# A tensor kept in DRAM between two passes: rows by feature, or blocks by tokens

## The chip, the core and the metric

The kernel runs on one core of one Trainium2 chip. The metric is the device time of one launch in microseconds (us), as the median of the runs shown. The engines are named as the profile names them: PE (TensorE, matmuls) with PEld (its weight loads), DVE (VectorE), ACT (ScalarE), POOL (GpSimd), SP (SyncE, which here only issues DMAs).

## What is computed

The kernel computes a block's output and all of its gradients in one launch: a layer norm of x (2048 tokens, 512 features), a long convolution over the tokens whose kernel comes from a state-space model (128 states per feature), a feed-forward network, and a gate.

```
xn = layernorm(A_u)
s  = causal_conv(xn, K) + xn * Dskip        # K from A, B, C, dt; by FFT in the reference
h  = xn @ w1                                # 2048 x 1792
o  = silu(h) @ w2                           # 2048 x 512
y  = A_u + s * silu(o)
outputs: y, and the gradients of A_u, A, B, C, log_dt, Dskip, w1, w2 for a given grad_out
```

What matters here is h, the inner tensor of the feed-forward network. It is made in the forward pass and needed twice more in the backward pass: its silu' for dh, and silu(h) for the gradient of w2. All inputs and outputs are bf16.

## The kernel before

h is 2048 x 1792 in bf16, 7.3 MB. It is too much to keep beside the rest, so it goes to DRAM, in the tensor `Hd`. With features on the partitions, h consists of FT = 14 row blocks of 128 features (`ft`), and its 2048 tokens are taken in eight chunks (`c`) of 256. `Hd` has the shape [14, 128, 2048]: for one row block and one partition, all 2048 tokens lie in one run of 4096 bytes. Four places touch it:

- **The store** (`gen_ffn_fwd`, line 1403). The forward network goes over the eight chunks. In each, 14 row blocks of `ps_h` are computed by matmuls and copied into `hT`, first eight blocks, then six. After each part ACT makes `aT` = silu(`hT`) for the second matmul (`ps_o`), and POOL issues the store of `hT` (`k.st` is `nc.gpsimd.dma_start`). A store writes, for every partition, 8 or 6 runs of 256 tokens, which is 512 bytes each. `hT` is single-buffered for each of the two parts.
- **The loads for da** (`gen_ffn_da`, line 1708). They read the same parts back into `dhT`, again in 512-byte runs; ACT replaces them by silu'(h), DVE multiplies by `ps_da`, and the product goes to DRAM as `DHd` and, as weights, into the matmuls `ps_dx`. Three buffers of eight row blocks and two of six allow loading ahead.
- **The plain loads for the gradient of w2** (`gen_dw2`, line 1764), eleven of the 14 row blocks. One load brings a row block with all its 2048 tokens into `h_in`, one run of 4096 bytes per partition. PE transposes it in 16 pieces of 128 x 128 (`pt_t`), ACT applies silu into `a_tok`, and 16 matmuls (`ps_w2`, shown as `ps_w<-YD,a_tok`) sum over the tokens.
- **The transposing loads** of the same stage (line 1762), for ft = 9, 11, 13. The DMA transposes [128, 2048] into `h_in`, and PE has no part in it.

`h_in` has two buffers; `load(ft + 2)` is recorded while ft is worked on. Its pool `fw` takes memory that the da stage (pools `wt` and `da`) uses before.

`DHd`, the stored dh, already has the shape [8, 128, 14, 256], with each partition's rows of a chunk contiguous, and `dh_tok<-DHd` reads it back with a transposing DMA whose source is [1024, 256].

All loads and the transposes go through SP's queue, in order; the stores of h, `Od` and most outputs go through POOL's.

The order of the work on each engine is not the order of the code. The functions only record operations; the class `Plan` then lays out a schedule from costs of its own. `backward` gives every operation a latest start; `forward` lets each engine take, among what is ready, the operation with the earliest one; the resulting list per engine is fixed by `tie`. `FIRST` and `LAST` hold its five settings: how long before its latest start a DMA may be issued (`hold`, ns), how far ACT may reach past an operation that needs another table (`table`) and PE past one of another tile shape (`turn`), the reluctance to use the slower of two possible engines (`shy`), and the time from a DMA's last byte to its landing (`land`). `ROUNDS` passes of the two refine it, `FROM` seeds the first, and `NUDGES` shifts the latest starts of chosen operations by pseudo-random amounts: 630 entries of seed, kind and size, found by a search that was done before the kernel was written down.

```
if "DMA" in kind or "Dma" in kind:
    ...
    run = min(self.run(a) for a in (aps[0], aps[1])) * 2
    packets = total / run
    each = 7.6 + run / 24.4 if run > 1024 else 25 if run <= 256 else 30.8 if run <= 512 else 48
    issue = (540.0 if packets <= 512 else 900.0) if eng == "Pool" else 600.0 if total < 200000 and run == 512 else 330.0 if packets <= 256 else 400.0
    return issue, packets * each / 16
...
self.lead = [400.0 + (c[0] if e == "Pool" else min(c[0], 330.0)) for c, e in zip(self.cost, self.eng)]
...
line = max(line, t + self.lead[n]) + l      # in forward, for a DMA
done[n] = line + land
```

Of the kernel before, what the change touches and what calls it, by code (L numbers as in the profile page):

```python
# [20 lines left out]
P = 128  # L21
# [159 lines left out]
class Plan:  # L181
# [5 lines left out]
    FROM, ROUNDS = (649172052, 1, 0), 5  # L187
    FIRST, LAST = (30000.0, 1500.0, 1500.0, 120.0, 3500.0), (30000.0, 1500.0, 1500.0, 120.0, 3500.0)
    NUDGES = [(2732807006, 5, 2000), (3483623756, 4, 500), (36678232, 7, 1000), (3625006935, 3, 100), (1835227684, 0, 100),
# [1190 lines left out]
def gen_ffn_fwd(k):  # L1380
    nc, fp = k.nc, k.fp
    D, FT, DK, T = k.D, k.FT, k.DK, k.T
    for c in range(T // 2):
# [3 lines left out]
        for f in range(FT // 2):  # L1387
# [12 lines left out]
            if f in (3, 6):  # L1400
                f0, n = (0, 8) if f == 3 else (8, 6)
                nc.scalar.activation(out=aT[:, f0:f0 + n], in_=hT[:, 0:n], func=ACT.Silu)
                k.st(k.Hd[f0:f0 + n, :, cs].rearrange("f p n -> p f n"), hT[:, 0:n])
# [668 lines left out]
```

## Time and profile before

| | |
|---|---|
| time of the runs, median of 3 | 562.91 us (562.78 to 563.13) |
| profiled execution, its time | 562.31 us |
| its span, first to last instruction | 560.6 us |
| mean granted TensorE clock | 0.991 |
| busy: PE, DVE, ACT, POOL | 515.5, 508.1, 432.0, 69.4 us |
| DMA packets | 178,882, 137.77 MB |

The profile is of one execution. Its stages, by what PE does: to about 42 us the layer norm, the tables and the constants; to 200 us the forward network together with the convolution forward; to 250 us the end of the convolution, the gates and the start of the backward pass; to 380 us the convolution backward together with da and dx; to about 450 us the state-space gradients; from 412 us on the weight gradients, first of w2 and then of w1, with the layer norm's backward pass. All operations are recorded by one helper, so every row carries the same line number, 171, and the tile's name tells what it is. "busy" of PE is taken from pipelined matmuls with modelled ends. A wait is put down to what came last. The chain of waits is followed back from the last instruction; a stage in which two engines are equally full can appear in it under either.

### The profile page before, as it was taken

Reading aid. Unit: us, or ns where it says so; the run is one execution under the profiler, and the core shown is the slowest. Engines: PE = TensorE matmul, PEld = TensorE weight load, DVE = VectorE, ACT = ScalarE, POOL = GpSimd, SP = SyncE. Lnnn points to the kernel's source line nnn. Section 1 sums busy time; section 2 is a strip of 40 time slices with the busy share of each in tenths; the row PEclk is TensorE's granted clock in tenths of the full one; section 3 lists DMA queues with packets and bytes.
Section 4 is the critical chain, followed back from the end, with each engine's and each line's share of the span. In section 5 each row is a group of like instructions: output and inputs, shape, how many; then the busy total and the mean of one; then the engine's idle time right before and its main releaser. Section 6 shows DMA issues by size and latency. Waiting matters only on the chain.

```text
span 560.6 us, 14249 instructions
## 1 busy us (share of the span) xinstructions
PE 515.5 (92%) x5820; PEld 380.5 (68%) x5820; DVE 508.1 (91%) x866; ACT 432.0 (77%) x726; POOL 69.4 (12%) x138
## 2 busy tenths in 40 slices
PE   1698999999989997889999999999969999999997
PEld 1465677868657666565877667778657687778775
DVE  9989999999999799999999999649999999999932
ACT  8989899999989889989878878247367665785621
POOL 5131111100100100000000100000000303301142
PEclk9999999999999998999999999999989999999999
DMA  8996959997999999985498997997999999998893
GB/s 236 270 354 179 291 191 337 246 335 155 237 350 280 359 337 218 236 208 169 156 236 295 252 329 234 188 264 180 229 254 241 227 237 277 256 229 217 200 233 109
DMA packets 178882, 137.77 MB, mean 246 GB/s; under 512 B 125121, under 2 KB 158657, under 8 KB 176257
## 3 DMA queue, kind: packets, MB, share of 16 engines
q1 hardware_dynamic: 172384, 118.77, 82.5%
q0 software_dynamic: 6144, 17.83, 9.6%
q8 instruction: 45, 0.74, 0.5%
q10 hardware_dynamic: 288, 0.26, 0.2%
q14 instruction: 21, 0.16, 0.1%
HBM read 50.07 MB, written 56.63 MB: 190 GB/s over the span
## 4 chain that ended last, share of the span: by engine, by line
PE 58%; DVE 16%; ACT 13%; DMA 8%; issue 3%; SPq 2%; POOL 0%; DVEq 0%; ACTq 0%; POOLq 0%
PE ps_w L171 18%; PE ps_da L171 8%; PE ps_i L171 7%; PE ps_dx L171 6%; DMA dB<-dA 4%; PE ps_s L171 4%; PE ps_o L171 3%; ACT mag_all L171 3%; PE ps_h L171 3%; PE pt_t L171 3%; PE psS L171 3%; PE ps_v L171 2%; ACT dA L171 2%; DVE AR L171 2%; DVE dA L171 2%
## 5 line engine op out<-in xcount | busy, mean ns | idle before, releaser
L171 PEld LDWEIGHTS <-W 128*128 128x128 bf16 x952 | 88.1, 99 | 22.9 <-issue 7.4
L171 ACT CAST dA<-ps_s 128x512 bf16<-128x512 f32 x160 | 86.2, 641 | 9.2 <-PE ps_s L171 6.3
L171 PE MATMUL ps_o<-W,aT 128*128 128x512 bf16 x224 | 59.0, 379 | 2.9 <-ACT aT L171 2.9
L171 PEld LDWEIGHTS <-xn 128*128 128x128 bf16 x512 | 47.3, 99 | 20.1 <-DVE xn L171 13.0
L171 PE MATMUL ps_da<-doT,W 128*128 128x256 bf16 x448 | 59.7, 273 | 0.8 <-DVE doT L171 0.8
L171 PE MATMUL ps_h<-XT,W 128*128 128x256 bf16 x448 | 58.9, 277 | 1.3 <-DVE dA L171 0.8
L171 PE MATMUL ps_w<-YD,a_tok 128*128 128x512 bf16 x224 | 57.5, 382 | 0.0
L171 PE MATMUL ps_w<-dh_tok,xn 128*128 128x256 bf16 x448 | 57.1, 273 | 0.0
L171 ACT CAST Vb<-ps_v 128x336 bf16<-128x336 f32 x109 | 40.6, 459 | 21.2 <-PE ps_v L171 15.5
L171 PE MATMUL ps_dx<-W,dhT 128*128 128x512 bf16 x224 | 55.2, 379 | 0.0
L171 ACT CAST dB<-ps_i 128x512 bf16<-128x512 f32 x82 | 45.3, 647 | 4.5 <-PE ps_i L171 4.3
L171 DVE TENSOR_TENSOR dhT<-ps_da,dhT 128x512 bf16<-128x512 f32 x56 | 37.8, 685 | 6.1 <-PE ps_da L171 5.9
L171 PEld LDWEIGHTS <-TF 128*128 128x128 bf16 x416 | 28.5, 100 | 12.5 <-ACT TF L171 5.3
L171 PEld LDWEIGHTS <-YD 128*128 128x128 bf16 x576 | 28.4, 98 | 9.0 <-DVE YD L171 1.7
L171 PEld LDWEIGHTS <-dhT 128*128 128x128 bf16 x224 | 20.7, 98 | 20.1 <-issue 1.2
L171 PEld LDWEIGHTS <-a_tok 128*128 128x128 bf16 x224 | 21.3, 99 | 16.9 <-issue 0.5
L171 PEld LDWEIGHTS <-aT 128*128 128x128 bf16 x224 | 19.4, 98 | 19.5 <-ACT aT L171 3.4
L171 PE MATMUL ps_v<-Gb,YT 128*128 128x168 bf16 x256 | 31.1, 242 | 1.3 <-DVE Gb L171 0.7
L171 ACT CAST o<-ps_w 128x512 bf16<-128x512 f32 (+1 forms) x27 | 15.1, 559 | 20.9 <-PE ps_w L171 20.4
L171 PE MATMUL ps_s<-dB,F 128*64 128x512 bf16 x192 | 28.6, 400 | 2.8 <-DMA dB<-dA 1.7
L171 POOL DMA_DIRECT2D out_dram<-o x20 | 12.3, 616 | 142.8 <-ACT o L171 135.0
L171 ACT ACTIVATE sn<-AR 128x1920 bf16<-128x1920 int16 x16 | 28.7, 1870 | 0.0
(218 smaller groups left out, 1212.9 us busy)
## 6 DMA issues: line engine op xcount, KB each, us to landing
Yd<-YD SPq DMA_DIRECT2D x8, 1024.0 KB, 6.5
h_in<-Hd SPq DMA_DIRECT2D x11, 512.0 KB, 5.5
Ed<-E SPq DMA_DIRECT2D x8, 672.0 KB, 4.3
Eb<-Ed SPq DMA_DIRECT2D x8, 672.0 KB, 5.4
Hd<-hT POOLq DMA_DIRECT2D x8, 512.0 KB, 5.7
dhT<-Hd SPq DMA_DIRECT2D x8, 512.0 KB, 5.4
DHd<-dhT SPq DMA_DIRECT2D x8, 512.0 KB, 6.9
Md<-mag_all SPq DMA_DIRECT2D x8, 480.0 KB, 6.4
```

Of the source, the lines that this page charges most:

```text
L171: getattr(getattr(nc, engine), op)(*[on(a) for a in args], **{w: on(a) for w, a in kw.items()})
```

## The change

`Hd` becomes [8, 128, 14, 256]: eight chunks of 256 tokens, and in each chunk every partition's 14 rows lie one behind the other (7168 bytes). This is the shape that `DHd` has. A store writes one run of 4096 or 3072 bytes per partition, and the loads for da read the same. A plain load for the gradient of w2 reads, per partition, eight runs of 512 bytes, one from each chunk. A transposing load reads 1024 rows of 256 tokens as two halves, so that block t of 128 tokens stands at t % 2 * 8 + t // 2 in `h_in`; the matmul's index follows. No compute instruction is added or taken away.

The plan's constants are others throughout. `hold` goes from 30000 to 22000, `table` from 1500 to 0, `land` from 3500 to 2700; `turn` and `shy` stay; `ROUNDS` goes from 5 to 8, and the list of nudges from 630 entries to 445, all different. So every engine's order is a new one.

```diff
-    FROM, ROUNDS = (649172052, 1, 0), 5
-    FIRST, LAST = (30000.0, 1500.0, 1500.0, 120.0, 3500.0), (30000.0, 1500.0, 1500.0, 120.0, 3500.0)
-    NUDGES = [(2732807006, 5, 2000), (3483623756, 4, 500), (36678232, 7, 1000), (3625006935, 3, 100), (1835227684, 0, 100),
...
+    FROM, ROUNDS = (3259356336, 0, 0), 8
+    FIRST, LAST = (22000.0, 0.0, 1500.0, 120.0, 2700.0), (22000.0, 0.0, 1500.0, 120.0, 2700.0)
...
@@ gen_ffn_fwd
-        cs = slice(256 * c, 256 * c + 256)
...
-                k.st(k.Hd[f0:f0 + n, :, cs].rearrange("f p n -> p f n"), hT[:, 0:n])
+                k.st(k.Hd[c, :, f0:f0 + n], hT[:, 0:n])
@@ gen_ffn_da
-        nc.sync.dma_start(dh[:, 0:n], k.Hd[f0:f0 + n, :, 256 * c:256 * c + 256].rearrange("f p n -> p f n"))
+        nc.sync.dma_start(dh[:, 0:n], k.Hd[c, :, f0:f0 + n])
@@ gen_dw2
-            nc.sync.dma_start_transpose(h[:], k.Hd[ft])
+            nc.sync.dma_start_transpose(h[:].rearrange("p (w c) n -> p w (c n)", w=2), k.Hd[:, :, ft].rearrange("c p n -> (c p) n"))
...
-            nc.sync.dma_start(h[:].rearrange("p t n -> p (t n)"), k.Hd[ft])
+            nc.sync.dma_start(h[:].rearrange("p (c w) n -> p c (w n)", w=2), k.Hd[:, :, ft].rearrange("c p n -> p c n"))
...
-            nc.tensor.matmul(out=ps[:], lhsT=at[:, t, :], rhs=k.do[:, t, :], start=(t == 0), stop=(t == k.T - 1))
+            nc.tensor.matmul(out=ps[:], lhsT=at[:, t % 2 * 8 + t // 2 if by_dma(ft) else t, :], rhs=k.do[:, t, :], start=(t == 0), stop=(t == k.T - 1))
@@ body
-    k.Hd = dr.tile([k.FT, P, L], BF16, name="Hd")
+    k.Hd = dr.tile([8, P, k.FT, 256], BF16, name="Hd")
```

More of the change, by code (lines that the diff above doesn't have):

```diff
@@ L186 @@
     SHY = 40.0
-    FROM, ROUNDS = (649172052, 1, 0), 5
-    FIRST, LAST = (30000.0, 1500.0, 1500.0, 120.0, 3500.0), (30000.0, 1500.0, 1500.0, 120.0, 3500.0)
-    NUDGES = [(2732807006, 5, 2000), (3483623756, 4, 500), (36678232, 7, 1000), (3625006935, 3, 100), (1835227684, 0, 100),
[125 rows of a table removed]
+    FROM, ROUNDS = (3259356336, 0, 0), 8
+    FIRST, LAST = (22000.0, 0.0, 1500.0, 120.0, 2700.0), (22000.0, 0.0, 1500.0, 120.0, 2700.0)
+    NUDGES = [(3008085398, 5, 200), (1251273428, 4, 500), (824357316, 4, 100), (2656081652, 4, 500), (2237630934, 4, 100),
[88 rows of a table added]
     def __init__(self, nc, tc, free):
```

213 rows, old and new, of the table NUDGES are left out of this document.

## The prediction

> **What bounds the kernel now.** I read the page first, then the busy time by stage, then the chain of waits, then the waits, and last the DMA issues, which is where the change is.
>
> ```profile
> span 560.6 us, 14249 instructions
> PE 515.5 (92%) x5820; PEld 380.5 (68%) x5820; DVE 508.1 (91%) x866; ACT 432.0 (77%) x726; POOL 69.4 (12%) x138
> ...
> q0 software_dynamic: 6144, 17.83, 9.6%
> ...
> PE 58%; DVE 16%; ACT 13%; DMA 8%; issue 3%; SPq 2%; POOL 0%; DVEq 0%; ACTq 0%; POOLq 0%
> ```
>
> TensorE is busy 92% of the span and VectorE 91%, so no single engine sets the time everywhere. The busy time by stage (columns: stretch, length, then PE, PEld, DVE, ACT and POOL busy, the granted clock, the share of the 16 DMA engines, GB/s) tells which one does where:
>
> ```profile
> 98.00:154.00 56.00, 55.25 (x746) 41.54 (x743) 55.74 (x73) 55.08 (x95) 4.57 (x6) 1.00 0.98 244
> ...
> 250.00:320.00 70.00, 69.18 (x886) 48.68 (x884) 68.54 (x93) 61.63 (x109) 5.01 (x10) 1.00 0.78 217
> 320.00:380.00 60.00, 60.00 (x665) 43.81 (x664) 44.63 (x70) 34.54 (x52) 1.71 (x4) 1.00 0.97 259
> 380.00:412.00 32.00, 30.20 (x293) 22.38 (x292) 32.00 (x51) 16.81 (x45) 0.00 (x0) 1.00 0.96 214
> 412.00:450.00 38.00, 34.57 (x361) 25.73 (x359) 35.67 (x57) 26.51 (x59) 4.86 (x9) 0.96 1.09 240
> 450.00:500.00 50.00, 49.99 (x499) 37.61 (x497) 50.00 (x107) 33.07 (x62) 12.01 (x22) 1.00 1.09 247
> 500.00:540.00 40.00, 40.00 (x357) 30.57 (x355) 36.23 (x87) 22.59 (x36) 7.23 (x12) 1.00 0.87 203
> ```
>
> From 250 to 540 us PE idles 0.82 + 0 + 1.80 + 3.43 + 0.01 + 0 = 6.1 us of 290. There a new order can win little and lose much. Most of those 6.1 us lie around 410 to 418, where the forward h comes back for the weight gradient. Earlier, at 98 to 154, three engines are full at once (55.25, 55.74 and 55.08 of 56), and an order has as little to gain there. The five longest DMA pieces of the chain are
>
> ```profile
> 33.75 7.33 DMA mag<-Md
> 56.38 8.63 DMA dB<-dA
> 141.87 13.64 DMA dB<-dA
> 199.22 7.36 DMA Gr<-in_grad_out_dram
> 410.73 6.32 DMA h_in<-Hd
> ```
>
> and of what PE itself lost to DMAs the waits name only two kinds:
>
> ```profile
> PE pt_t L171 <- DMA h_in<-Hd: 3.4, 2, 3.2
> ...
> PE pt_f L171 <- DVE dA L171: 3.3, 1, 3.3
> ...
> PE ps_s L171 <- DMA dB<-dA: 1.7, 2, 1.4
> ```
>
> (The middle row is no DMA; a rival needs it below.) Of the tensor that the change lays out anew, only the weight-gradient loads stand on the path; neither its stores nor the loads for da do.
>
> **The stores of h (16, from POOL).** In the tile view of `hT` and `Od` (ns min/median/max):
>
> ```profile
> L171 POOL DMA_DIRECT2D Hd<-hT x16: 831/891/1089, 32.2 to 190.6; - x16
> L171 POOL DMA_DIRECT2D Od<-ob x8: 555/567/567, 49.0 to 217.2; - x8
> ```
>
> and in the waits:
>
> ```profile
> POOL Hd L171 <- ACT hT L171: 79.2, 10, 21.1
> ```
>
> A store goes from 512-byte runs (one per partition and 128-row of h) to one run per partition, as `Od<-ob` has. I price it at that neighbour: 16 x (0.89 - 0.57) = 5.1 us less POOL work. POOL stands idle 79.2 us before these very stores and holds 0% of the chain, so the saving is worth 0. As for the packets, the software queue's row gives 17.83 MB / 6144 = 2.9 KB a packet, although 7.3 MB of it are the 16 stores of h, whose 512-byte runs alone would be 14,336 packets: those stores already travel in large packets, and here the change removes nothing from the DMA engines. Bounds: 0.3 us either way, if a store that ends sooner or later moves the reuse of the single-buffered `hT`; no wait in the trace names it. Value 0.
>
> **The loads for da (16) and for dW2 (11 plain).** The tile views have them at
>
> ```profile
> L171 SPq DMA_DIRECT2D dhT<-Hd x16: 377/430/1589, 231.6 to 375.9; - x16
> ```
>
> ```profile
> L171 SPq DMA_DIRECT2D h_in<-Hd x11: 338/523/572, 410.2 to 504.2; - x11
> ```
>
> Two stretches of the DMA view in which practically one size runs give its price (packets, MB, share of 16 engines): 232.5 to 235 us, where the 512-byte packets of `dhT` run, and 415 to 416 us, where the 4096-byte packets of `h_in` run.
>
> ```profile
> q1 hardware_dynamic: 1288, 0.65, 89.8%
> ```
>
> ```profile
> q1 hardware_dynamic: 97, 0.39, 97.9%
> ```
>
> 2.5 us x 16 x 0.898 / 1288 = 27.9 ns for 512 bytes; 1 us x 16 x 0.979 / 97 = 161 ns for 4096 bytes, where eight small ones take 223 ns. A load of 512 KB is 128 x 161 / 16 = 1.29 us of all engines in large packets and 1024 x 27.9 / 16 = 1.79 us in small ones: 0.5 us between them. The change trades one for the other. The da loads (7.3 MB, fourteen halves' worth of 512 KB) win 14 x 0.5 = 7 us of engine time between 231 and 376 us; the eleven loads of dW2 lose 11 x 0.5 = 5.5 us between 410 and 505 us.
>
> The gain lands where nobody waits: no engine's wait names `dhT<-Hd`, and PE is full at 320 to 380 us for reasons of its own. Value 0, at best -0.5 us through shorter queues. The loss lands in the stages with a DMA share of 1.09. Its cover is that `h_in` is loaded two row blocks ahead; the first load has no such cover, because it is issued only when the memory of the da stage is free (410.2 us), and PE waited 3.2 us for it. That one grows by its 0.5 us; if both of the first two count, 1.0. Against this stand the issue rows:
>
> ```profile
> h_in<-Hd SPq DMA_DIRECT2D x11, 512.0 KB, 5.5
> dhT<-Hd SPq DMA_DIRECT2D x8, 512.0 KB, 5.4
> dh_tok<-DHd SPq DMA_TRANSPOSE x14, 6.0
> h_in<-Hd SPq DMA_TRANSPOSE x3, 7.8
> ```
>
> The same 512 KB landed in 5.4 us in small packets and in 5.5 in large ones, so the effect may be 0. I take +0.5, with 0 to +1.0 for the range. SP's own time is not at stake: an issue took 430 ns in small packets and 523 in large ones, and nothing queued behind it on SP moves by more than that 0.1 us.
>
> [...]
>
> **The three transposing loads of h (ft 9, 11, 13).** They get exactly the form that `dh_tok<-DHd` has: rows of 256 tokens, eight blocks. That form landed in 6.0 us, the old one in 7.8 (three samples). The consumer changes only the index with which it picks a block of 128. So -0.5 to +0.5; value 0, since the nearest row says it is no worse and none of the three shows a wait of PE.
>
> [...]
>
> **The new order.** This is the part with the widest price: every engine's queue is a different one, and the constants that made it differ. Two matter. The time that a DMA is given after its transfer until it counts as landed goes from 3500 to 2700 ns, and ScalarE's window for putting off an instruction that needs another table goes from 1500 ns to 0. With the old constant a 512 KB load of `h_in` is given 0.73 us for the issue, about 1.4 for the transfer and 3.5, together 5.6 us; the trace's median is 5.5. The new constant gives it 4.8. So work that hangs on a DMA is placed about 0.8 us too early, and on engines that take their queue in order everything behind it waits too. Of the five long pieces above, two are `dB<-dA`, for which PE waits already: 2 x 0.8 = 1.6 us. I leave out `h_in` (its load goes when room comes free, whatever the plan says) and the two for which only VectorE waits. Bounds: one piece 0.8, all five 4.0; a gain is not excluded and is priced below. The table window could add loads, by
>
> ```profile
> L171 ACT ACT_TABLE_LOAD x10 | 12.8, 1283 | 1.4 <-PEq L2056 1.2
> ```
>
> at 1.28 us each, felt in full at 98 to 154 us where ACT is busy 55.08 of 56 us. The ten seen belong to the few changes between the phases, so I count none.
>
> **Sum.** Profiled execution 562.31 us (span 560.6 and 1.7 around it), 0.6 below the median of 562.91. Stores 0, da loads 0, first `h_in` +0.5, transposes 0, order +1.6: 564.4 on the profiled execution, 565.0 on the median. Own range of this case: 562.91 + 0.8 to 562.91 + 1.0 + 4.0, so 563.7 to 567.9.
>
> **Rivals.** *The order closes the hole at 410 to 418 us (faster).* Columns as above:
>
> ```profile
> 218.00:224.00 6.00, 3.31 (x32) 3.33 (x32) 4.64 (x9) 5.94 (x9) 0.00 (x0) 0.63 1.07 262
> 224.00:230.00 6.00, 5.38 (x38) 2.27 (x36) 5.82 (x9) 5.02 (x10) 0.00 (x0) 0.80 1.21 243
> ```
>
> ```profile
> 414.00:418.00 4.00, 1.97 (x28) 1.80 (x29) 4.00 (x6) 1.77 (x3) 0.00 (x0) 0.94 1.13 319
> 418.00:422.00 4.00, 4.00 (x28) 2.82 (x26) 2.01 (x5) 2.05 (x6) 0.00 (x0) 0.64 0.99 152
> ```
>
> PE waits 3.4 us there and then runs at half clock for a while: 4 x 0.06 + 4 x 0.36 = 1.7 us lost. A plan that ends the da stage, and with it the use of its memory, sooner, or that keeps 3.4 us of the state-space part's matmuls for this moment, gets up to 5.1 us: 557.8. With half of it, 560.4. It decides once PE has over 1.1 us of other work ready at 412. Against it: VectorE, which makes that work, is full at 380 to 412 (32.00 of 32). For it: it is one wait at one place, and the da loads' lighter packets leave the queue emptier before it.
>
> *The order opens another such hole (much slower).* The pattern at 216 to 230 us is the price: PE waits 3.3 us for `dA`, then 6 x 0.37 + 6 x 0.20 = 3.4 us go to the clock. One more of these in 250 to 540, where nothing absorbs it: 562.91 + 6.7 = 569.6, with the h_in term 570.6.
>
> *Nothing that can be measured.* The layout shifts 7 us of engine time one way and 5.5 the other, both hidden; the orders come out even. 562.9, inside 561.8 to 564.0 (0.2%, or 1.1 us, is about what a measurement of this kernel tells from no change).
>
> **Chances.** Forecast 0.38, much slower 0.17, faster 0.34, even 0.11. The layout itself is worth little by every row, so the sign hangs on the order; it leans to slower, as PE has 6.1 us to win and no floor below it after 250 us. Slower by over 0.2%: 0.38 + 0.17 = 0.55. The range goes from the full price of the faster rival, 557.8, to that of the much slower one, 570.6; I leave some 0.15 outside.
>
> **What would show it.** Right: POOL's stores of h at about 0.57 us; some 14,300 small packets fewer and 11,300 more; the `h_in` wait at about 3.7 us or longer; the waits of PE on `dB<-dA` above 1.7 us; PE busy time equal and its idle time 2 us more. [...]

## The result: 1.2% slower, and where the profile after has it

The changed kernel takes 569.99 us (566.54 to 571.11, four runs) against 562.85 us (562.6 to 563.13): a ratio of 1.0116, 95% interval 1.0072 to 1.016 (ratios go by all runs; the quotient of the two medians would be 1.0127). On another chip it was 566.8 against 560.11 us, 1.0113 (1.0076 to 1.015). The profiled execution of after took 569.6 us, with a span of 567.9, a clock of 0.991 as before, and 176,193 DMA packets.

The page of after, in the lines that answer to those of before:

```profile
span 567.9 us, 14246 instructions
PE 520.1 (92%) x5820; PEld 378.8 (67%) x5820; DVE 502.5 (88%) x855; ACT 434.0 (76%) x737; POOL 63.9 (11%) x138
q1 hardware_dynamic: 169952, 118.77, 80.9%
q0 software_dynamic: 5888, 17.83, 8.9%
PE 50%; DVE 19%; ACT 9%; DMA 9%; issue 8%; SPq 3%; POOL 0%; DVEq 0%; ACTq 0%; POOLq 0%
```

PE stands idle 567.9 - 520.1 = 47.8 us, 2.7 more than before (45.1), and is busy 4.6 us longer with the same 5,820 matmuls. The half clock cannot be what makes it longer, as it lasts 10.2 us in both traces (6.83 and 3.41 us in each); what does is not shown. But the longer of its stretches lies at 315 us now and lay at 219 before. The busy time by stage, in the same stretches as before (columns: stretch, length, then PE, PEld, DVE, ACT and POOL busy, the granted clock, the share of the 16 DMA engines, GB/s):

```profile
250.00:320.00 70.00, 66.94 (x846) 46.12 (x843) 67.21 (x91) 60.05 (x105) 3.21 (x6) 0.97 0.68 191
320.00:380.00 60.00, 60.00 (x659) 43.22 (x658) 40.72 (x59) 35.50 (x54) 3.50 (x7) 0.98 0.95 270
380.00:412.00 32.00, 29.14 (x286) 22.23 (x285) 30.80 (x49) 20.18 (x53) 0.00 (x0) 1.00 0.96 196
412.00:450.00 38.00, 34.01 (x364) 25.14 (x362) 37.69 (x59) 26.53 (x60) 4.26 (x8) 0.96 1.13 242
```

From 250 to 320 us there are now 3.06 us of idle PE where there were 0.82, and a clock of 0.97 where it was 1.00. The fine windows of after show what that is; in the first three of them before has PE busy all the time at full clock.

```profile
306.00:313.00 7.00, 7.00 (x74) 4.76 (x73) 7.00 (x10) 5.75 (x8) 1.86 (x4) 1.00 0.78 169
313.00:317.00 4.00, 1.04 (x7) 0.19 (x5) 3.65 (x6) 2.95 (x5) 0.27 (x1) 0.80 1.20 252
317.00:322.00 5.00, 5.00 (x32) 3.38 (x31) 0.69 (x1) 1.17 (x2) 0.00 (x0) 0.50 0.89 251
315.41:322.24 6.83, 6.00 (x37) 3.81 (x38) 1.93 (x4) 1.71 (x4) 0.00 (x0) 0.50 0.98 244
```

The last line is the whole stretch at half clock. PE stands still for 2.96 us, to 316.25 us; the clock falls at 315.41, while it still waits, and stays at half until 322.24, so PE works at half clock for 6.0 us. This hole is new. Its cause is in the queue of SP, here from its timeline (start, duration of the issue, operation):

```profile
297.70 0.45 SPq L171 DMA_DIRECT2D DHd<-dhT  x1
298.26 0.36 SPq L171 DMA_DIRECT2D go_x<-in_A_u_dram  x1
307.03 0.33 SPq L171 DMA_DIRECT2D dhT<-Hd  x1
307.77 8.44 SPq L171 DMA_TRANSPOSE dB<-dA  x2
```

The waits of SP's queue at 285 to 320 us (who waited for what: us, times, longest) name it,

```profile
SPq L171 <- DMA DHd<-dhT: 13.7, 2, 8.4
```

and the waits of PE the consequence, with a second, smaller one that an experiment below takes up:

```profile
PE ps_s L171 <- DMA dB<-dA: 3.0, 1, 3.0
...
PE G L171 <- issue: 1.7, 1, 1.7
```

The load `dhT<-Hd` writes a buffer that the store `DHd<-dhT` of 297.70 us still reads, so SP waits for that store to land, about 307 us. The plan had given it 6.8 us (293.39 to 300.19 in its own times); it took 9.3. The two transposing loads `dB<-dA` have nothing to do with either, but they stand behind on the same queue. What they do need, the last copies into `dA`, was there earlier:

```profile
302.07 3.18 ACT L171 CAST dA<-ps_s 128x512 bf16<-128x512 f32 x6
```

These end at 305.25 us, and the loads go out at 307.77, 2.5 us later. The plan has no such delay: in it the store lands just before the copies end, and the transposing loads go out at 300.78, when both are done. So the plan let SP wait for the store, and the 2.5 us by which the store landed late became 2.5 us of delay for the loads behind it. The matmuls `ps_s` wait for these loads.

For the changed tensor itself, the tile view of `hT` has (ns min/median/max of an issue)

```profile
L171 POOL DMA_DIRECT2D Hd<-hT x16: 537/539/807, 29.9 to 199.7; - x16
```

and the DMA issues have (the last number is the median from issue to landing):

```profile
h_in<-Hd SPq DMA_DIRECT2D x11, 512.0 KB, 6.3
dhT<-Hd SPq DMA_DIRECT2D x8, 512.0 KB, 5.1
dh_tok<-DHd SPq DMA_TRANSPOSE x14, 6.5
h_in<-Hd SPq DMA_TRANSPOSE x3, 6.1
```

The stores cost POOL 0.54 instead of 0.89 us each, the plain `h_in` loads land in 6.3 instead of 5.5 us, the transposing ones in 6.1 instead of 7.8. Which of this the layout does and which the order, the next section separates.

### The profile page after: what moved, and what is told of

It reads as the page before. It is cut to its first block, busy times and chain, and to the rows that moved or that the text cites. A ratio compares the mean times of both kernels' runs of the same rounds, so it can differ in the third digit from the quotient of the medians.

```text
span 567.9 us, 14246 instructions
## 1 busy us (share of the span) xinstructions
PE 520.1 (92%) x5820; PEld 378.8 (67%) x5820; DVE 502.5 (88%) x855; ACT 434.0 (76%) x737; POOL 63.9 (11%) x138
## 2 busy tenths in 40 slices
DMA packets 176193, 137.77 MB, mean 243 GB/s; under 512 B 125120, under 2 KB 155584, under 8 KB 173568
## 3 DMA queue, kind: packets, MB, share of 16 engines
q1 hardware_dynamic: 169952, 118.77, 80.9%
q0 software_dynamic: 5888, 17.83, 8.9%
## 4 chain that ended last, share of the span: by engine, by line
PE 50%; DVE 19%; ACT 9%; DMA 9%; issue 8%; SPq 3%; POOL 0%; DVEq 0%; ACTq 0%; POOLq 0%
PE ps_w L171 15%; PE ps_da L171 8%; PE ps_dx L171 7%; PE ps_i L171 6%; DVE AR L171 4%; PE ps_s L171 3%; PE ps_v L171 3%; SPq L171 3%; ACT mag_all L171 3%; PE psS L171 3%; DVE W L171 2%; DVE YD L171 2%; DVE dA L171 2%; PE pt_t L171 2%; ACT dA L171 2%
## 5 line engine op out<-in xcount | busy, mean ns | idle before, releaser
L171 ACT CAST dA<-ps_s 128x512 bf16<-128x512 f32 x161 | 88.0, 678 | 3.7 <-PE ps_s L171 2.9
L171 PE MATMUL ps_h<-XT,W 128*128 128x256 bf16 x448 | 61.3, 278 | 2.8 <-DVE XT L171 1.4
L171 PE MATMUL ps_dx<-W,dhT 128*128 128x512 bf16 x224 | 58.1, 385 | 0.5 <-ACT Vb L171 0.5
L171 PE MATMUL ps_w<-YD,a_tok 128*128 128x512 bf16 x224 | 55.4, 379 | 0.0
L171 PE MATMUL ps_w<-dh_tok,xn 128*128 128x256 bf16 x448 | 54.3, 273 | 0.0
L171 ACT CAST Vb<-ps_v 128x336 bf16<-128x336 f32 x123 | 46.1, 480 | 9.7 <-PE ps_v L171 8.0
L171 ACT CAST o<-ps_w 128x512 bf16<-128x512 f32 (+1 forms) x25 | 13.6, 554 | 29.1 <-PE ps_w L171 28.6
L171 PEld LDWEIGHTS <-dhT 128*128 128x128 bf16 x224 | 20.9, 99 | 20.3 <-issue 3.8
L171 PE MATMUL ps_s<-dB,F 128*64 128x512 bf16 x192 | 30.4, 396 | 4.0 <-DMA dB<-dA 3.0
L171 ACT ACTIVATE dhT<-dhT 128x2048 bf16<-128x2048 bf16 (+1 forms) x16 | 28.0, 1771 | 7.5 <-DMA dhT<-Hd 6.4
L171 PEld LDWEIGHTS <-aT 128*128 128x128 bf16 x224 | 19.9, 98 | 19.9 <-issue 3.8
L171 PEld LDWEIGHTS <-ident 128*128 128x128 bf16 x388 | 25.4, 99 | 10.0 <-issue 3.4
```

Source lines behind the costliest of these rows:

```text
L171: getattr(getattr(nc, engine), op)(*[on(a) for a in args], **{w: on(a) for w, a in kw.items()})
```

## Experiments

Every ratio is to runs of the kernel before on the same chip, with its 95% interval. Times in us in the first four expectations are those of the first chip, where before took 562.9 us; on the chip of these runs it took 560.11, so the ratios are what can be compared. "Old order" is that of before, "new order" that of the changed kernel. Where one order is put on the other layout, the plan is made from its own record and constants and then emitted on the other layout, so every engine's queue is the same.

**One half of the change at a time.**

```diff
 # new_layout_old_order: before's constants and nudges, Hd and its five uses as in the changed kernel
-    k.Hd = dr.tile([k.FT, P, L], BF16, name="Hd")
+    k.Hd = dr.tile([8, P, k.FT, 256], BF16, name="Hd")
 # old_layout_new_order: the changed kernel's constants and nudges, Hd as before
```

> h in eight blocks, but every engine's order is that of the kernel before, instruction by instruction (the plan is made from the old layout and then carried out on the new one). If the order costs the 7 us and the layout next to nothing: 562.4 to 564.0 us, against 562.9 before; POOL's stores of h at about 0.56 us instead of 0.89; the loads of h_in 0 to 0.5 us later. If the layout costs them (small packets into the crowded stage after 410 us): 567 to 571. If both must fit each other: between 564 and 567.

> The other way about: h in rows by feature as before, every engine's order that of the changed kernel. If the order costs the time: 567 to 571 us, with the hole of PE at 313 to 322 us still there. If the layout does: 562 to 564. If both must fit each other: over 571, since the new order was searched on the new layout.

> The changed kernel itself beside the others on the same chip, for its spread: 566.5 to 571.1 in four runs so far. 569 to 571 as median; if the hole at 313 us depends on the phase of something outside the program, single runs at about 566 again.

Measured: layout alone 1.0054 (1.0034 to 1.0075), order alone 1.0129 (1.009 to 1.0167), both 1.0113. The order alone gives the whole loss. The layout costs 3.0 us on the old order, and on the new one nothing that shows (1.0113 against 1.0129, intervals overlapping). So the two do not add up. By the ratios (1.0054 and 1.0129 times 562.9 are 565.9 and 570.2 us) the first run fell into the expectation's range for layout and order that must fit each other, and the second into that for an order that costs the time.

The landing of the three transposing loads of h, in new_layout_old_order and in old_layout_new_order,

```profile
h_in<-Hd SPq DMA_TRANSPOSE x3, 7.6
h_in<-Hd SPq DMA_TRANSPOSE x3, 6.1
```

shows that their 6.1 instead of 7.8 us comes with the order and not with the layout. The plain loads land in 6.5 and 5.3 us there, so their delay comes with the layout.

**The store in front of the queue.** Operation 4124 is the store of `dh`, 4145 the first of two transposing loads on SP ahead of it in the changed kernel's plan.

```diff
+    store, ahead_of = 4124, 4145
+    for line in (plan.best.sequence, plan.best.plan["SP"]):
+        line.remove(store)
+        line.insert(line.index(ahead_of), store)
```

> The changed kernel with one DMA moved on SP's queue: the store of dh that the load of dhT at 307 us waits for is issued ahead of two transposing loads dB<-dA instead of behind nine other issues, so the load finds its buffer free and the next two transposes are not held behind it. If the hole of PE at 306 to 322 us comes from that wait on SP: SP's wait on DHd<-dhT falls from 14.4 us in all to under 3, PE's 3.0 us wait for dB<-dA and the half-clock stretch at 315 us go, 564 to 566 us. If the transposes were held by their own data (the copies on ACT) or by the DMA engines: at most 1 us better, 569 to 570.

Measured: 1.0083 (1.0055 to 1.0112). PE's waits for `dB<-dA` fall from 3.0 to 0.7 us in the whole launch, none of it in the old hole, and the stretch that showed the hole is full (same columns):

```profile
306.00:313.00 7.00, 7.00 (x98) 4.66 (x95) 7.00 (x11) 7.00 (x10) 0.54 (x1) 1.00 0.78 149
313.00:317.00 4.00, 4.00 (x38) 2.73 (x36) 4.00 (x6) 3.22 (x5) 1.59 (x3) 1.00 1.02 246
```

The copies into `dA` and the transposing loads are in this trace at

```profile
303.69 3.18 ACT L171 CAST dA<-ps_s 128x512 bf16<-128x512 f32 x6
306.90 6.56 SPq L171 DMA_TRANSPOSE dB<-dA  x2
```

so the loads go out as soon as their data is there (306.87 us) and no longer 2.5 us behind it. They also take 6.56 instead of 8.44 us; why is not isolated. The hole's cause is shown by this. Two things did not come out as expected: SP still waits 5.7 us for `DHd<-dhT` and not under 3, 4.1 of it for another load of `dhT`, which goes out at 297 us, and 1.0083 is about 567.6 us on the first chip, between the two ranges. How much of the launch time the hole is worth is less sure, as the interval overlaps with that of the unmoved kernel. To see where the rest is, I put the traces on a common scale: the durations of all matmuls at full clock, as the kernel's own `cost_of` has them, added up in the order in which their weights are loaded, come to 484.1 us in every kernel. (From some traces 53 to 56 matmul records are missing; the weight loads are all there, so the marks are set by them.) The table gives the time that each trace takes from one mark of this scale to the next, and in the second column when before reaches the mark (us).

```
        at   before  NL     S     B     H     C     T  | after again  OL    ST   ST+h  ST+c  ST+GE
  0    5.3     82.1  81.4  81.7  81.4  82.1  82.2  81.9 |  82.6  82.7  83.0  82.6  84.0  82.6  82.7
 60   87.4    116.3 114.6 116.2 114.6 116.3 116.5 115.5 | 119.3 119.0 119.4 118.9 118.6 119.3 119.0
165  203.7     45.2  45.1  44.8  47.3  45.4  46.3  44.2 |  39.3  40.0  41.2  41.2  41.1  39.3  41.0
195  248.9     66.4  65.4  66.4  65.3  65.3  65.3  66.4 |  64.8  64.8  64.8  65.1  65.2  65.1  65.2
255  315.2     16.5  16.5  16.5  16.5  16.5  16.5  16.5 |  22.5  20.2  20.6  16.6  16.6  16.6  16.6
270  331.8     60.7  60.7  60.9  60.7  60.7  60.7  60.7 |  61.3  61.3  61.3  61.3  61.3  61.3  61.3
330  392.5     17.1  17.1  17.1  17.1  17.1  17.1  17.1 |  19.2  19.2  19.5  19.9  19.7  20.2  18.0
345  409.6     21.1  18.9  22.0  18.3  19.5  22.9  22.4 |  21.5  20.4  19.6  20.3  20.3  20.0  23.9
360  430.7     46.0  48.0  47.6  46.8  46.7  47.1  46.0 |  46.1  46.1  46.4  46.1  46.6  51.2  46.1
405  476.7     76.5  76.5  76.5  76.5  76.5  76.5  76.5 |  77.8  76.5  76.5  77.9  76.5  76.5  77.6
NL new_layout_old_order, S old_order_small_reads, B old_order_large_reads, H old_order_h_in_ahead,
C old_order_chain_sooner, T old_order_two_moves, OL old_layout_new_order, ST store_of_dh_earlier,
ST+h new_order_two_moves, ST+c new_order_store_and_chain, ST+GE new_order_store_and_GE
```

Rows 60 and 165 (87 to 249 us): the new order first loses 2.8 and then wins 4.2 us by the medians; mark 255 it reaches 1.3 us sooner (at 313.1 against 314.4 us, medians of seven traces each). The gain is the hole of before at 216 to 226 us, which the prediction used as a price: its wait of 3.3 us for `dA` is not among the waits of after, nor is the half-clock stretch of 219 us. Row 255: it takes 3.7 to 6.0 us longer, and 16.6 us against 16.5 once the store is moved. Row 330: it takes 19.2 to 20.2 us for 17.1, until the last experiment. In row 345 both orders spread over more than 4 us, with half-clock stretches that fall there or not, and no cause is read from it.

**Which part of the layout costs.** The plain `h_in` loads alone are given the other packet size. Both kernels read other rows of h, so the gradient of w2 is computed from those.

```diff
 # old_order_small_reads: flat layout, 8 runs of 512 bytes
-            nc.sync.dma_start(h[:].rearrange("p t n -> p (t n)"), k.Hd[ft])
+            nc.sync.dma_start(h[:].rearrange("p (c w) n -> p c (w n)", w=2), k.Hd[0:8, :, 256 * (ft % 8):256 * (ft % 8) + 256].rearrange("f p n -> p f n"))
 # old_order_large_reads: blocks, one run of 4096 bytes
-            nc.sync.dma_start(h[:].rearrange("p (c w) n -> p c (w n)", w=2), k.Hd[:, :, ft].rearrange("c p n -> p c n"))
+            nc.sync.dma_start(h[:].rearrange("p t n -> p (t n)"), k.Hd[ft % 8, :, 0:8].rearrange("p f n -> p (f n)"))
```

> The kernel before, order and layout of h untouched, but each of the eleven plain loads of h_in reads 8 runs of 512 bytes per partition (tokens of eight row blocks, so the gradient of w2 is computed from other rows) in place of one run of 4096 bytes. Theory A, the small packets of these loads are what the new layout costs on the old order (1.0054 there): 1.003 to 1.007 of before, h_in landing 6.3 to 6.7 us instead of 5.5, and waits for several later h_in loads, 3 us or more in all. Theory B, the cost comes from the layout's other parts (stores, da loads, transposing loads): 0.998 to 1.002, waits for h_in as before (3.4 us of the matmuls, two waits). Theory C, chance stretches of half clock: 1.000, and the next kernel too.

> The new layout on the order of before, as in new_layout_old_order (1.0054), but each plain load of h_in reads one run of 4096 bytes per partition (eight row blocks of one chunk, so the gradient of w2 is computed from other rows). Theory A (small packets of h_in): 0.997 to 1.002, h_in landing back at 5.4 to 5.7 us and one long wait for the first h_in as before. Theory B (other parts of the layout): 1.003 to 1.007 as with the small reads. Theory C (chance half clock): 1.000.

Measured, on one chip: small reads on the flat layout 1.0034 (1.0008 to 1.006), large reads on the new layout 0.9986 (0.9964 to 1.0007). The waits of PE for `h_in` over the whole span, with small reads

```profile
PE pt_t L171 <- DMA h_in<-Hd: 5.4, 5, 2.6
PEld L171 <- DMA h_in<-Hd: 7.0, 5, 2.7
```

and with large reads:

```profile
PE pt_t L171 <- DMA h_in<-Hd: 1.2, 2, 1.0
PEld L171 <- DMA h_in<-Hd: 2.5, 4, 1.1
```

Five waits of the matmuls instead of two: with small packets not only the first load is late, but later ones too (in new_layout_old_order 3.7 us in four waits). Row 360 of the table, where later loads of `h_in` fall, agrees: 48.0 and 47.6 us in the two kernels of the old order with small packets, 46.0 to 47.1 in the other five. The landing (median) is 6.3 us with small and 5.0 with large reads, 5.5 before; on the block layout with the old order alone it is 6.5 with small and 5.0 with large. Theory A holds; stores, da loads and transposing loads cost nothing that shows. One part of the expectation failed: the one long wait for the first load, 3.2 us before, did not come back with large reads (1.0 us is the longest there).

**The first h_in load sooner.** In the old order two loads of parameters stand ahead of it on SP.

```diff
 # old_order_h_in_ahead; 5227, 5228 load the parameters, 6092 is the second load of h_in
+    for line in (plan.best.sequence, plan.best.plan["SP"]):
+        for n in (5227, 5228):
+            line.remove(n)
+        at = line.index(6092) + 1
+        line[at:at] = [5227, 5228]
 # old_order_two_moves: this, and on DVE
+    for line in (plan.best.sequence, plan.best.plan["DVE"]):
+        for n in (6015, 6016):
+            line.remove(n)
+        at = line.index(5987) + 1
+        line[at:at] = [6015, 6016]
 # new_order_two_moves: store_of_dh_earlier, and YT's transposing loads 5928, 5929 behind 6092 in the same way
```

> The kernel before with one move on SP: the two transposing loads of parameters, issued at 406.5 and 408.8 us and first used at 438 us, go behind the first two loads of h_in, which wait only for the last ps_dx (ended 407.2 us) and were issued at 410.15. Theory: PE's hole at 412 to 416 us is made by the order of issues on SP, so h_in is issued 2 to 2.9 us sooner, the hole shrinks by as much, and with the half-clock stretch behind it gone another 1.7 us: 557.3 to 560 by a before of 562.3, a ratio of 0.992 to 0.9965. Rival: VectorE, full from 380 to 418 us, sets the pace there and the hole opens elsewhere: 0.999 to 1.001.

> The kernel before with the parameters' loads behind the first two h_in loads, as in old_order_h_in_ahead (1.0002), and on VectorE the two steps g_u<-g_z,Sa and g_z<-g_z,Sa (0.69 us each) moved from between the products at 415 and 418 us to the idle 2.0 us at 419 to 421. If VectorE sets the stage and h_in no longer waits, 1 to 2.5 us come off: 0.9955 to 0.9985. If not, 1.000.

> The changed kernel with two moves on SP: the store of dh as in store_of_dh_earlier (1.0083), and the two transposing loads of YT that stand ahead of the first two h_in loads go behind them. In the changed kernel h_in was issued 2.8 us after the last ps_dx ended (419.9 against 417.1). Theory, holes made by SP's order are what the new order costs: 1 to 2.5 us off, 1.004 to 1.0065. Rival, the matmuls there wait for VectorE (Tp, 2.7 us) whatever h_in does: 1.0075 to 1.009, as without the second move.

Measured: 1.0002 (0.9978 to 1.0026), 1.0002 (0.998 to 1.0024), and 1.009 (1.0062 to 1.0118) against 1.0083 without the second move. Nothing gained three times, although the load did go sooner. From SP's timeline of old_order_h_in_ahead

```profile
406.36 0.81 SPq L171 DMA_DIRECT2D h_in<-Hd  x2
407.22 1.15 SPq L171 DMA_TRANSPOSE par<-in_A_A_re_dram  x1
```

and from its waits of PE at 404 to 430 us:

```profile
PE pt_t L171 <- DMA h_in<-Hd: 2.1, 2, 1.1
PE ps_v L171 <- ACT Vb L171: 1.2, 1, 1.2
```

The wait for `h_in` falls from 3.4 to 2.1 us, and a new wait for `Vb` takes up 1.2. In old_order_two_moves the two loads go out at 405.24 us, and PE still waits for `h_in`:

```profile
PE pt_t L171 <- DMA h_in<-Hd: 3.3, 2, 2.1
```

My theory of this hole was wrong by that: it is not the order of issues alone that makes it. In new_order_two_moves PE still waits 3.7 us for `Tp`, as the rival there had it.

**Is it VectorE?** Nine steps of the state-space parameters' gradients (`g_z`, `g_u`, `gout`) lie between the products `Tp` and `Tq` in the new order and behind them in the old.

```diff
 # old_order_chain_sooner: one step behind each of the nine DVE operations that follow 6016
+    chain = [6017, 6018, 6020, 6021, 6022, 6023, 6098, 6097, 6099]
+    for n, m in zip(chain, behind):
+        seq.remove(n)
+        seq.insert(seq.index(m) + 1, n)
 # new_order_store_and_chain: the store moved, and 6017, 6018 and all that hangs on them goes to 426 us of the plan
+    rest = [n for n in seq if n not in group]
+    seq[:] = rest[:at] + moved + rest[at:]
+    for line in best.plan.values():
+        line.sort(key=place.get)
```

> The kernel before with the same nine steps moved the other way, from behind the products Tp and Tq to between them, as the new order has them. Theory (VectorE sets the end of the stage at 393 to 431 us): 2 to 4 us more, 1.003 to 1.008, and the stage takes 2 us or more longer. Rival (PE and DMAs set it): 0.999 to 1.001.

> The changed kernel with the store of dh moved as in store_of_dh_earlier (1.0083) and, besides, nine steps of the state-space parameters' gradients (g_z, g_u, gout; 4.6 us of VectorE, which the new order puts between the products Tp and Tq at 416 to 431 us and the old one only after them) moved behind those products, with what hangs on them. Theory, from 393 to 431 us VectorE is full and sets the end, so whatever is put into that stage is paid: it lasts 39.0 to 40.7 us in the new order and 35.4 to 38.2 in the old; 2 to 4 us come off, 1.002 to 1.006. Rival, the stage is long because of what PE and the DMAs do there, and VectorE follows: 1.0075 to 1.0095.

Measured: putting the chain in costs the old order 1.0038 (1.0008 to 1.0067), as expected. The stage itself (rows 330 and 345) takes 40.0 us for 38.2 in before's trace, which the spread of row 345 in the old order cannot tell from chance. Taking it out of the new order gave 1.0157 (1.0118 to 1.0196), worse than either theory. The table's rows 330 and 345 did not shorten (20.2 + 20.0 us, with the store alone 19.9 + 20.3), and behind them the move made a hole of its own, in the waits of PE at 431 to 446 us:

```profile
PE pd L171 <- DVE g_u L171: 4.2, 1, 4.2
```

The matmul `pd` was put right behind the chain that feeds it, in the list that the plan fixes for PE, and PE stood still before it for these 4.2 us. So in the old order work put between the products is paid by the total, though the traces do not show where, and that this is what the new order loses there is not shown.

**The load of GE.** The rival of the last two, PE and a late load, was left: in row 330 the idle time stands before the matmuls `G`, and their last load goes out on SP behind two transposing loads and three stores.

```diff
 # new_order_store_and_GE: the store moved, and 5456, the last load of GE, ahead of 5428, a transposing load
+        line.remove(5456)
+        line.insert(line.index(5428), 5456)
```

> The changed kernel with the store of dh moved as in store_of_dh_earlier (1.0083) and, besides, the last of four loads of GE put right behind the third on SP, ahead of two transposing loads of YT, a store of Pd and two of dh (it was issued at 391.3 us there, 7 us behind the third, and the matmuls G began at 397.3 after 2.3 us in which PE stood still). In all five traces of the new order so far the matmuls that take 17.1 us in the old order from 392.5 us on take 19.2 to 20.2 us, and 1.7 to 2.3 of it is this idle time. Theory, the idle time is SP's late issue and PE sets the end there: those matmuls take 17.0 to 18.0 us, 1.0035 to 1.006. Rival, VectorE, busy 38.6 of 39.7 us in this stage, sets the end, and PE only stands still elsewhere: 1.0075 to 1.009.

Measured: 1.0037 (1.001 to 1.0064), against 1.0083 with the store alone. Row 330 falls to 18.0 us. The wait of PE at 385 to 433 us with the store alone

```profile
PE G L171 <- issue: 2.3, 1, 2.3
PE G L171 <- DMA GE<-dKd: 0.8, 1, 0.8
```

is not in the waits of this kernel any more; there the two loads go out together:

```profile
383.51 1.25 SPq L171 DMA_DIRECT2D GE<-dKd  x2
```

Two DMA instructions, moved up by ten and by five places on one queue, take back 1.13 - 0.37 = 0.76 points of the 1.13%; the intervals of the two kernels do not overlap. About 0.4% stays, within 0.1 to 0.6. Open there are the 0.6 us of row 270, the wait of PE for `Tp` in 345 (3.5 us in after; the waits of before have 0.5 there), the 1.1 to 1.4 us of row 405 in three of the seven traces, and what small packets cost on this order. With both holes closed, PE has a wait for the loads in small packets that it did not have in after:

```profile
PE pt_t L171 <- DMA h_in<-Hd: 1.8, 1, 1.8
```

No kernel tried was faster than before beyond its interval.

## Why the prediction was right in its sign and wrong in its size

The measured 570.0 us lies inside the range of 557.8 to 570.6, at its far end; the own range of the likeliest case ended at 567.9. What came about is the rival *much slower*, which had 0.17: one more hole of PE between 250 and 540 us with a half-clock stretch behind it, priced at 6.7 us. In after's trace it is 3.0 us of waiting and 6.0 us of work at half clock, 3.0 + 3.0 = 6.0, which is what row 255 has (22.5 against 16.5). The price counted the half clock also while PE stood still; before's own stretch (columns as in the table of stages)

```profile
219.53:226.36 6.83, 5.67 (x44) 4.26 (x46) 5.43 (x9) 6.20 (x7) 0.00 (x0) 0.50 1.06 217
```

gives 3.3 + 2.8 = 6.1. That the total came so near this one price is luck in part: in changed_kernel_again, with 1.0113 as the ratio of its runs, the hole costs 3.7 us and has no half clock, the second hole adds 2.1 us that the rival did not have, and the hole of 216 to 226 us is gone.

**The stores: right.** 0.54 us instead of 0.89, POOL 5.5 us less busy, and worth nothing (old_order_large_reads, which has these stores, is at 0.9986). After's chain does have one store of h, 5.24 us from 84.73 us on, but no engine's wait names it.

**The loads for da: right.** They land in 5.1 instead of 5.4 us (4.6 in new_layout_old_order), and row 270, the da stage, is 60.7 us on the old order with either layout.

**The plain h_in loads: mis-sized.** The term was +0.5 us, up to 1.0. On the old order it is 1.9 us by old_order_small_reads (0.0034 x 561.3, from 0.4 to 3.4) and 3.0 by new_layout_old_order. The packets' price was right in kind; the step that failed is the cover, "loaded two row blocks ahead", and with it that the first load alone grows: the longest wait did not grow (2.6 us, 3.2 before), and five waits instead of two show that the cover is thin for later loads. The loads themselves land in 6.5 us in small packets and in 5.0 in large ones, on the same order and layout (new_layout_old_order and old_order_large_reads). On the new order the term is not seen: none of PE's waits in after names `h_in`. The first load goes out at 419.9 us, and PE then waits for `Tp` until 424.3; row 360 is 46.1 us in after with small packets and 46.1 in old_layout_new_order with large ones. That it is hidden there rather than gone is what the 1.8 us in new_order_store_and_GE suggest, in one trace. So the sign "h_in wait of 3.7 us or longer" did not come, and its absence was no gain.

**The transposing loads: right.** On the same order the new form lands in 7.6 us and the old one in 7.8, three samples each; the 6.1 of after is the order's doing.

**The order: the step that failed.** +1.6 us stood for 7.2 (old_layout_new_order, 0.0129 x 560.1). I had multiplied 0.8 us of `land` by the two `dB<-dA` pieces of the old chain, at 56 and 142 us. Neither is in the long pieces of after's chain; the wait is on another `dB<-dA`, at 308 us. From the chain of waits of after (start, length, piece):

```profile
298.26 8.48 DMA go_x<-in_A_u_dram
307.77 8.43 DMA dB<-dA
```

(The chain names the load that goes out right behind the store and lands at 306.7 us; SP's own waits name the store.) A landing that the plan puts too early was indeed the beginning (6.8 us planned, 9.3 taken), and that "everything behind it waits too" stands in the prediction; but 0.8 us of `land` is a third of those 2.5, and I had priced it at the loads which PE waited for before. What I did not price is SP's own queue: there a load that waits for a buffer holds up unrelated transposing loads. Before, that queue waited 0.8 us for `DHd<-dhT`, in after 14.4. The second hole, `GE`, lies on the same queue (7.6 us between the last two loads with the store alone, where the plan has 4.5; which wait in between does it is open), and neither could be read from the trace of before. The bound of 4.0 us for the order was drawn from pieces that already existed, which is the reason that it was too low.

**The other signs.** The wait of PE for `dB<-dA` rose from 1.7 to 3.0 us and table loads are ten, as said. Idle PE: 2.7 us more, where 2 were said. PE's busy time was to stay equal and is 4.6 us longer. Half-clock stretches after 250 us: two in after (315 and 425 us), one before, and none in changed_kernel_again. Packets: on the queue of SP 172,384 became 169,952, which is 12,288 fewer for da and 9,856 more for `h_in`, as the run lengths give. The faster rival did not come: from 412 to 450 us PE is busy 34.0 us where it was 34.6.

## What to carry to other kernels

On a queue taken in order, a DMA that must wait for a buffer is a wait for everything behind it (on SP in after, 2.5 us for two transposing loads whose data was there); before an order is changed, list for each issue that waits for a buffer what stands behind it, and put the loads that an engine is about to need ahead of it. Price a new order from what its queues can block, not from the holes that the old order shows. A layout that makes packets large for one reader and small for another is worth what the reader on the path loses (1.9 us with the small reads alone), and in this kernel on the old order, where the DMA share is 1.09 from 412 to 450 us, two loads of look-ahead did not hide packets of 512 bytes: PE waited 5.4 us for them, in five waits, and in before, with packets of 4096, 3.4 us in two.

## What the runs showed of the hardware

**Half clock hits the same hole or not.** In after PE stood still for 2.96 us, and after 2.1 of them the clock fell to 0.50 for 6.8 us; in changed_kernel_again it stood still 3.52 us at the same place and the window behind it shows

```profile
317.00:322.00 5.00, 4.80 (x48) 3.09 (x49) 1.59 (x3) 2.05 (x4) 0.00 (x0) 1.00 0.97 235
```

Row 255 of the table has both, 22.5 and 20.2 us. Inside the spans of before and after there are two such stretches each, of 6.83 and 3.41 us; what sets their start and length is not shown. A single trace's total says little here, its stages do: the traced run of new_order_store_and_GE is the slowest of its twelve (561.1 to 566.4 us). That the half clock makes this spread is not shown; before spreads as much beside it (558.8 to 564.3).

**Which packets a store of POOL makes.** Its stores of h had 512-byte runs before and 4096 or 3072 after, yet its queue's packets only fell from 6,144 to 5,888, and the 512 KB land in 5.6 us instead of 5.7; only the issue got cheaper (0.54 us instead of 0.89). On SP's queue the same change of run length made 2,048 packets for da out of 14,336: in old_order_large_reads, where the plain h_in loads keep their runs of 4096 bytes, that queue has 160,096 packets, 12,288 fewer than the 172,384 of before.
